# Attention turned MoE layer on one core: q of chunks 2 and 3 turned by the DMA crossbar, transposes in two halves, loads planned behind them, and token statistics summed over whole rows

## The chip, the cores and the metric

The kernel runs on one core of a Trainium2 chip. A core has a matrix engine (TensorE, PE in the profile) with its weight loads (PEld), a vector engine (VectorE, DVE), an activation engine (ScalarE, ACT), a general engine (GpSimd, POOL) and a queue engine (SyncE, SP). They run side by side, each through its own list of instructions in order, and wait for each other through semaphores. Sixteen DMA engines move data; loads here are issued on POOL (queue q0), stores and transposes on SP (queue q1). Matrix products go to PSUM, which has eight banks; everything else lies in SBUF. The metric is the time of one execution on the device in microseconds (us).

## The reference

```python
kv  = einsum('bhsd,bhse->bhde', k, v)           # b=8, h=8, s=576, d=64
o   = einsum('bhsd,bhde->bhse', q, kv)
x   = o / sqrt(mean(o*o, -1) + 1e-6) * g_norm   # per head; then [4608 tokens, 512]
h   = x @ w_in                                  # 512 -> 1024
u   = h * softmax(h)
ln  = (u - mean(u)) / sqrt(var(u) + 1e-6) * g_ln
out = ln @ w_out                                # 1024 -> 512
```

Inputs and output are float32. The layer norm needs, for each token, the mean of u, of u*u, and of exp(h), which is the softmax's divisor.

## The kernel before

The 4608 tokens are cut into nine chunks of 512. Chunk c, for c from 0 to 7, is the first 512 tokens of batch c; chunk 8 takes the last 64 tokens of all eight batches. All work on a chunk has the tokens in the columns and the features in the partitions:

1. The loads of k, v and q of a batch (`load_kv` L216, `load_q` L223), issued on POOL, cast to bfloat16 on the way. Chunks 0 and 1 load in two groups of heads, later chunks in one DMA each for k, v and q. The tiles have three buffers each. `load_q_last` (L229) fetches the last 64 tokens of a batch's q for chunk 8.
2. `kv_mm` (L278): 48 matmuls for k'v of all heads, into a bank of tag `misc`, of which there is one; four casts (L291, L293) copy the result to `kvd`, twice.
3. q has to be turned, so that head dimensions lie in the partitions. Chunks 0 to 3 do this on TensorE (`qT_mm` L301, a group of eight transposes for each half of the heads, followed by a copy out of PSUM, L310 or L308). Chunks 4 to 8 (`XBAR`, L124) are turned by the crossbar of the DMA engines (`q_turn` L315), with one instruction for all eight heads, issued on SP.
4. `o_mm` (L330) for each half of the heads, then a square, a mean over the head by TensorE (`s_mm` L351), logarithm and exponential on ACT (L355, L359) and the product x (L372, DVE).
5. `h_mm` (L449): eight groups of four 512-column matmuls; for each an exp (L457, ACT), u (L464, DVE) and u squared (L475 on POOL or L473 on ACT); for each pair of groups the sum of two exps, `es` (L481, POOL).
6. `sums` (L515): for the token statistics TensorE multiplies u, u squared and es with a column selector `stat_sel` of 32 columns, and adds them up over the features. The 128x128 array is used as four tiles of 32 columns. Each tile adds up its own 128 tokens: 20 sources of 512 columns, cut in four, make 80 matmuls of 128 columns. `sums_turn` (L523) turns the 128x128 result in 32x32 blocks within the same bank, `stats` (L531 to L536) forms the variance and `rstd` (L540, L542) its inverse root.
7. `out_mm` (L563): eight groups of four matmuls, for each of four blocks of 128 tokens two groups (halves of the features), into banks of tag `out` (two of them; `o` in part of chunk 8). `scale` (L573 DVE, L571 ACT) multiplies by rstd and `store` (L582) writes 256 KB from SP, from a tile `ob` with four buffers.

The order of the work is not written out as loops. Every piece is added to a `Plan` (L19) with its engine, an estimated length, a rank, the pieces that it needs and the buffers that it uses. `Plan.order` (L33) takes, again and again, the piece that could start earliest by those estimates (ties by rank), and the instructions are issued in that order, engine by engine. It models the load queue (`queue`, `lanes`) and the tiling in which TensorE stands; a change of tiling costs 0.1 us in it. The estimates decide the order alone; on the chip only semaphores for real data and buffers make an engine wait. In particular the list `behind` (L252) of a load names pieces of work that the load is planned after, although it shares no data with them: it decides where the load's instructions stand in POOL's list, and nothing more.

Before the change, the loads of chunk 3 are planned behind h_mm(0,2), and those of chunk b from 4 on behind h_mm(b-3,0). The lists that come out of it are quoted here as far as they are needed. On POOL: k_2 ... v_2 ... q_2 usq(0,5) k_3 v_3 es(0,1) q_3 es(0,2) es(0,3) k_4 v_4 q_4, then the twelve pieces of chunk 1 up to es(1,3), k_5 v_5 q_5 q_last(0), and further on k_6 behind es(2,3), k_7 behind es(3,3). On TensorE: kv_mm(3) stands behind h_mm(1,1), kv_mm(4) behind h_mm(2,3), kv_mm(5) behind h_mm(2,5), kv_mm(6) behind h_mm(3,4) and kv_mm(7) behind h_mm(4,4); o_mm(7,0) behind h_mm(5,6).

Of the kernel before, what the change touches and what calls it, by code (L numbers as in the profile page):

```python
# [8 lines left out]
FP32 = mybir.dt.float32  # L9
# [9 lines left out]
class Plan:  # L19
# [13 lines left out]
    def order(self):  # L33
# [3 lines left out]
        behind = {}  # L37
# [5 lines left out]
        while ready:  # L43
# [20 lines left out]
            if engine == "pe":  # L64

                tiling = n[0] if n[0] in ("kv_mm", "o_mm", "sums") else "full"
                length += 0.1 if mode.get(engine, tiling) != tiling else 0.0
                mode[engine] = tiling
            if n[0] == "qT" and engine == "sp":

                if queue > t + 1.0:
                    length, queue = 2.2 * length, queue + 2.0
            free[engine] = t + length
# [15 lines left out]
def kernel(  # L89
# [33 lines left out]
    banks = {"h": 2, "out": 2, "o": 2, "s": 1, "misc": 1}  # L123
    XBAR = tuple(range(4, NC))  # L124
    bufs = {
        "k": 3, "v": 3, "q": 3, "qT": 3, "osq": 4, "lss": 2, "rst": 2, "oc": 2, "x": 2, "e": 4, "u": 2, "usq": 2, "es": 2,
        "ob": 4,
    }
# [4 lines left out]
    def tile_of(key, shape, dtype):  # L133
        return sb.tile(shape, dtype, name=key[0] + "_sb", tag=key[0], bufs=bufs[key[0]])
# [20 lines left out]
    ident = big.tile([128, 128], BF16, name="ident")  # L155
    eye = big.tile([NF, NF], FP32, name="eye")
    zeros = big.tile([128, 512], BF16, name="zeros")
    nc.vector.memset(zeros, 0.0)  # L158
# [46 lines left out]
    def make_ident():  # L205
        make_identity(nc, ident)
        make_identity(nc, eye)

    plan.add("ident", "pool", 1.0, -1.95, make_ident)


# [38 lines left out]
    for b in range(B):  # L250
        at = b - 9.0 if b > 1 else (-2.0, -1.5)[b]
        behind = [] if b < 2 else [("h_mm", 0, 0)] if b == 2 else [("h_mm", b - 3, 2 if b == 3 else 0)]  # L252
        for g, hs in enumerate(heads(b)):
# [57 lines left out]

    def q_turn(c):

        t = T["qT", c] = tile_of(("qT", c), [128, H, 2, 128], BF16)
        nc.sync.dma_start_transpose(  # L315
            t.rearrange("q h y p -> q (h y) p"), T["q", c].rearrange("p h j d -> p (h j d)")
        )
# [61 lines left out]
    for c in range(NC):  # L379
# [14 lines left out]
        if c in XBAR:  # L394
            plan.add(("qT", c), "sp", 4.0, r - 0.1, lambda c=c: q_turn(c),
                     [("q", c, 0)] if c < B else [("q_last", b) for b in range(B)],
                     uses=[("q", c)] if c < B else [], first=[("qT", c)])
        for hf in range(2):
            g = group(c, hf)
            tag = ("out", "h")[c] if c < 2 and hf else "o"  # L400
            if c not in XBAR:
# [9 lines left out]
            plan.add(("o_mm", c, hf), "pe", 0.25 if c < B else 1.2, r + w * (0.35 + 0.5 * hf),  # L411
                     lambda c=c, hf=hf, tag=tag: o_mm(c, hf, tag), [("qT", c) if c in XBAR else ("qT", c, hf), *kvs],
                     uses=[("qT", c)], first=[(tag, c, hf, z) for z in range(2)])
# [92 lines left out]
    def sums(c, part):  # L506
        if part == 0:
            T["sum", c] = bank(("misc" if c else "h", "sum", c), [128, 2, 128], FP32)
        i, src = ((1, T["u", c]), (0, T["usq", c]), (2, T["es", c]))[part]
        n_src = NF // 2 if part == 2 else NF  # L510
        for n in range(n_src):
            for j in range(4):

                cols = src[:, n, :].rearrange("p (m j r) -> p j m r", m=4, j=4)[:, j]
                nc.tensor.matmul(  # L515
                    T["sum", c][32 * j:32 * j + 32, 0, :], stat_sel[:, i, :], cols, start=(part == 0 and n == 0),
                    stop=(part == 2 and n == n_src - 1), tile_position=(0, 32 * j), skip_group_check=True,
                )

    def sums_turn(c):  # L520

        T["st", c] = T["sum", c][:, 1, :].rearrange("p (m i) -> p m i", m=4)
        nc.vector.transpose(T["sum", c][:, 1, :], T["sum", c][:, 0, :])  # L523

    small = ctx.enter_context(tc.tile_pool(name="small", bufs=2))

    def stats(c):

        st = T["st", c]
        w = small.tile([128, 4, 3], FP32, name="w")  # L530
        nc.vector.tensor_tensor(out=w[:, :, 1:3], in0=st[:, :, 1:3], in1=factors[:, :, :], op=MUL)  # L531
        nc.vector.memset(w[:, :, 0:1], 1.0)
        terms = small.tile([128, 4, 3], FP32, name="terms")
        nc.vector.tensor_tensor(out=terms[:, :, :], in0=st[:, :, 0:3], in1=w[:, :, :], op=MUL)
        T["vare", c] = small.tile([128, 4], FP32, name="vare")
        nc.vector.tensor_reduce(out=T["vare", c][:, :], in_=terms[:, :, :], op=ADD, axis=mybir.AxisListType.X)  # L536
# [51 lines left out]
    for c in range(NC):  # L588
# [3 lines left out]
                 uses=[("u", c), ("usq", c), ("es", c)], first=[("misc" if c else "h", "sum", c)])  # L592
        plan.add(("turn", c), "dve", 0.25, rs + 0.14, lambda c=c: sums_turn(c), [("sums", c)],
                 uses=[("misc" if c else "h", "sum", c)])
        plan.add(("stats", c), "dve", 0.65, rs + 0.16, lambda c=c: stats(c), [("turn", c)], uses=[("misc" if c else "h", "sum", c)])
        plan.add(("rstd", c), "act", 0.45, rs + 0.17, lambda c=c: rstd(c), [("stats", c)])
# [45 lines left out]
```

## Time and profile before

| | |
|---|---|
| Time, median of 3 runs (lowest to highest) | 203.02 us (202.76 to 203.15) |
| The profiled execution, its own time | 203.15 us |
| Its span, first to last instruction | 201.3 us |
| PE, DVE, ACT, POOL busy | 89%, 60%, 70%, 64% |
| Granted TensorE clock | 1.0 throughout |
| HBM read, written | 32.51 MB, 9.44 MB |
| h_mm and out_mm, a group of four matmuls | 0.86 us in the chain |
| sums of a chunk (80 matmuls) | 1.23 us in the chain |
| transpose of a chunk by the crossbar, issue to landing | 3.6 to 6.6 us, median 3.9 |
| loads k, v, q of a whole chunk, issue to landing, medians | 11.8, 12.2, 13.8 us |

Times in the profile count from the first instruction. Busy time counts an engine's own instructions; issuing a DMA does not count on SP, and on POOL it does. A row of a timeline has start, length, engine, line, operation, tiles and count, and in brackets the idle time ahead of it with what ended it. A wait that hangs on several semaphores is put down to the one that came last by the profile; where the engine named had long been done, it was something else, often a DMA. The chain of waits is followed from the last instruction back: at each step to what released it, or to its predecessor on the same engine.

### The profile page before, as it was taken

What the parts mean: (1) busy time and instruction counts of PE and PEld (TensorE: products, weight loads), DVE (VectorE), ACT (ScalarE), POOL (GpSimd) and SP (SyncE); (2) the same over time, 40 slices, a digit from 0 to 9 for tenths busy, and PEclk for the clock granted to TensorE, in tenths of its full rate; (3) what the DMA queues carried; (4) which work ended last, traced back from release to release, by engine and by line L of the source; (5) the groups of instructions that cost most, each with busy time, mean ns of one, the idle gap of its engine ahead of it and who ended that gap; (6) DMA issues with size and microseconds to landing.
All of it is one profiled execution on the core that took longest, in us unless ns stands there. A gap on an engine that the chain in (4) does not pass through costs nothing.

```text
span 201.3 us, 5003 instructions
## 1 busy us (share of the span) xinstructions
PE 179.0 (89%) x2055; PEld 88.5 (44%) x2082; DVE 121.1 (60%) x232; ACT 140.9 (70%) x244; POOL 128.7 (64%) x137
## 2 busy tenths in 40 slices
PE   7987988797699889995999499999999999999990
PEld 2342444454354454453445244544545554454440
DVE  1246577468765758747484657586574748656440
ACT  2038887897698699885688558779697677655421
POOL 7962699602699984877497748397655738857200
PEclk9999999999999999999999999999999999999999
DMA  2999999999994999599849983137021111211205
GB/s 38 184 198 282 328 200 202 201 211 246 238 193 65 212 196 234 123 175 226 212 67 174 228 212 70 42 81 185 27 99 57 55 55 52 104 55 52 106 22 190
DMA packets 39990, 29.68 MB, mean 147 GB/s; under 512 B 11800, under 2 KB 34336, under 8 KB 39968
## 3 DMA queue, kind: packets, MB, share of 16 engines
q0 software_dynamic: 24208, 17.30, 56.0%
q1 hardware_dynamic: 15472, 11.54, 18.5%
q10 hardware_dynamic: 288, 0.52, 0.8%
q8 instruction: 16, 0.26, 0.5%
q14 instruction: 6, 0.05, 0.1%
HBM read 32.51 MB, written 9.44 MB: 208 GB/s over the span
## 4 chain that ended last, share of the span: by engine, by line
PE 55%; DMA 23%; ACT 7%; POOL 6%; issue 4%; DVE 3%; POOLq 0%; ACTq 0%
PE out_ps L563 22%; PE h_ps L449 20%; DMA v_sb<-in_v_dram 15%; DMA w_out_f<-in_moe_w_out_dram 9%; PE misc_ps L515 4%; PE o_ps L330 2%; PE s_ps L351 2%; PE misc_ps L278 2%; PE o_ps L563 2%; ACT e_sb L457 2%; POOL k_sb L216 2%; ACT rst_sb L359 1%; ACT lss_sb L355 1%; DVE u_sb L464 1%; ACT osq_sb L345 1%
## 5 line engine op out<-in xcount | busy, mean ns | idle before, releaser
L449 PE MATMUL h_ps<-x_sb,w_in_sb 128*128 128x512 bf16 x264 | 69.0, 379 | 2.2 <-DVE x_sb L372 1.2
L563 PE MATMUL out_ps<-w_out_sb,u_sb 128*128 128x512 bf16 x259 | 66.9, 379 | 1.4 <-issue 0.8
L481 POOL TENSOR_TENSOR es_sb<-e_sb 128x512 bf16<-128x512 f32 x36 | 45.7, 1270 | 34.5 <-ACT e_sb L457 34.3
L464 DVE TENSOR_TENSOR u_sb<-h_ps,e_sb 128x512 bf16<-128x512 f32 x69 | 47.3, 687 | 29.4 <-ACT e_sb L457 28.9
L475 POOL TENSOR_TENSOR usq_sb<-u_sb 128x512 bf16<-128x512 bf16 x51 | 52.6, 1042 | 18.5 <-DVE u_sb L464 18.2
L457 ACT ACTIVATE e_sb<-h_ps,zero_t 128x512 f32<-128x512 f32 x69 | 47.1, 685 | 15.3 <-PE h_ps L449 15.0
L449 PEld LDWEIGHTS <-w_in_sb 128*128 128x128 bf16 x288 | 27.3, 98 | 34.7 <-issue 3.6
L563 PEld LDWEIGHTS <-u_sb 128*128 128x128 bf16 x288 | 27.1, 98 | 32.4 <-issue 1.4
L372 DVE SCALAR_TENSOR_TENSOR x_sb<-o_ps,g_rep,rst_sb 128x512 bf16<-128x512 f32 x32 | 24.0, 750 | 9.3 <-ACT rst_sb L359 8.9
L573 DVE TENSOR_SCALAR ob_sb<-out_ps,rstd 128x512 f32<-128x512 f32 x33 | 24.4, 745 | 8.4 <-ACT rstd L542 4.7
L345 ACT ACTIVATE osq_sb<-o_ps,zero_t 128x512 bf16<-128x512 f32 x31 | 19.8, 682 | 7.6 <-PE o_ps L330 7.6
L359 ACT ACTIVATE rst_sb<-lss_sb,zero_t 128x512 f32<-128x512 f32 x32 | 23.3, 728 | 0.6
L355 ACT ACTIVATE lss_sb<-s_ps,eps_t 128x512 f32<-128x512 f32 x32 | 22.0, 688 | 0.8 <-PE s_ps L351 0.7
L473 ACT ACTIVATE usq_sb<-u_sb,zero_t 128x512 bf16<-128x512 bf16 x21 | 15.2, 722 | 5.4 <-DVE u_sb L464 5.2
L293 ACT CAST kvd<-misc_ps 64x128 bf16<-64x128 f32 (+1 forms) x24 | 7.5, 313 | 15.1 <-DVE kvd L291 10.8
L351 PE MATMUL s_ps<-osq_sb,head_mean 128*128 128x512 bf16 x34 | 12.9, 380 | 0.9 <-ACT lss_sb L355 0.6
L278 PE MATMUL misc_ps<-v_sb,k_sb 96*64 96x64 bf16 x384 | 8.0, 197 | 6.0 <-DMA v_sb<-in_v_dram 3.7
L515 PEld LDWEIGHTS <-stat_sel 128*32 128x32 bf16 x720 | 10.2, 97 | 4.3 <-issue 4.3
L278 PEld LDWEIGHTS <-k_sb 96*64 96x64 bf16 x384 | 7.1, 112 | 10.7 <-issue 10.7
L197 PE MATMUL s_ps<-zeros 128*128 128x512 bf16 x27 | 10.1, 502 | 1.6 <-DVE zeros L158 1.2
L223 POOL DMA_DIRECT2D q_sb<-in_q_dram x10 | 8.5, 853 | 3.5 <-DMA w_in_sb<-in_moe_w_in_dram 1.5
L291 DVE CAST kvd<-misc_ps 64x256 bf16<-64x256 f32 (+1 forms) x16 | 6.1, 382 | 6.8 <-ACT kvd L293 4.8
(80 smaller groups left out, 127.4 us busy)
## 6 DMA issues: line engine op xcount, KB each, us to landing
out_dram<-ob_sb SPq DMA_DIRECT2D x34, 256.0 KB, 2.5
k_sb<-in_k_dram POOLq DMA_DIRECT2D x6, 576.0 KB, 11.8
v_sb<-in_v_dram POOLq DMA_DIRECT2D x6, 576.0 KB, 12.2
q_sb<-in_q_dram POOLq DMA_DIRECT2D x6, 512.0 KB, 13.8
w_out_f<-in_moe_w_out_dram POOLq DMA_DIRECT2D x1, 2048.0 KB, 17.6
k_sb<-in_k_dram POOLq DMA_DIRECT2D x4, 288.0 KB, 12.4
v_sb<-in_v_dram POOLq DMA_DIRECT2D x4, 288.0 KB, 12.7
q_sb<-in_q_dram POOLq DMA_DIRECT2D x4, 256.0 KB, 12.7
```

What stands on the lines that cost most here:

```text
L278: nc.tensor.matmul(t[hh * 64:hh * 64 + 64, n, :], T["k", b][:, h, i, :], T["v", b][:, h, i, :], start=(n == 0 and i == 0), stop=(i == 5), ...
L345: nc.scalar.activation(out=t[:, :], in_=T[("o", *i)].rearrange("p a b c -> p (a b c)"), func=AF.Square, bias=zero_t[:, :])
L355: nc.scalar.activation(out=t[:, :], in_=T["s", i][:, :], func=AF.Ln, bias=eps_t[:, :])
L359: nc.scalar.activation(out=t.rearrange("p a b c -> p (a b c)"), in_=T["lss", i][:, :], func=AF.Exp, scale=-0.5, bias=zero_t[:, :])
L372: nc.vector.scalar_tensor_tensor(out=T["x", c][:, 2 * hf:2 * hf + 2, z], in0=T["o", c, hf, z][:, :, :, :], scalar=g_rep[:, :], in1=T["rst" ...
L449: nc.tensor.matmul(t[:, :], w_in_sb[:, dt, f * 128:(f + 1) * 128], T["x", c][:, dt].rearrange("p a b c -> p (a b c)"), start=(dt == 0), st ...
L457: nc.scalar.activation(out=T["e", c, f // 2][:, f % 2, :], in_=T["h", c, f][:, :], func=AF.Exp, bias=zero_t[:, :])
L464: nc.vector.tensor_tensor(out=T["u", c][:, f, :], in0=T["h", c, f][:, :], in1=T["e", c, f // 2][:, f % 2, :], op=MUL)
L475: nc.gpsimd.tensor_tensor(out=dst, in0=src, in1=src, op=MUL)
L481: nc.gpsimd.tensor_tensor(out=T["es", c][:, n, :], in0=e[:, 0, :], in1=e[:, 1, :], op=ADD)
L563: nc.tensor.matmul(T["acc", c, m][:, :], T["u", c][:, f, m * 128:(m + 1) * 128], w_out_sb[:, f, :], start=(f == 0), stop=(f == NF - 1),)
L573: nc.vector.tensor_scalar_mul(out=t[:, :], in0=T["acc", c, m][:, :], scalar1=T["rstd", c][:, m:m + 1])
```

## The change

It has three parts.

*Turning q.* `XBAR` begins at chunk 2 instead of 4, so the TensorE transposes and copies of chunks 2 and 3 fall away. Each crossbar transpose is cut in two, one for heads 0 to 3 and one for heads 4 to 7 (128x8x128 elements instead of 128x16x128), and `o_mm` of a half needs its own half alone. The planner's length of a transpose goes from 4.0 to 2.0 for a half, and one that meets a busy load queue now pushes that queue by its own length.

*The loads.* From chunk 3 on, the loads of chunk b are planned behind the first half of the transpose of chunk b-1, and, from chunk 4 on, h_mm(b-3,0).

*The statistics.* `sums` gives each of the four 32-column tiles whole sources of 512 columns in turn, 20 matmuls instead of 80. The four tiles then hold partial sums of the same tokens. `sums_turn` turns 128x512 in 32x32 blocks from PSUM to a new SBUF tile `sumT`, and a new piece `stats_mm` (`st_mm` in the plan) adds up the four parts: four float32 matmuls with 32 output rows and 12 columns each, with a constant `fold` of four stacked 32x32 identities. `stats` reads their bank, and so waits for TensorE once more.

```diff
             if n[0] == "qT" and engine == "sp":
                 if queue > t + 1.0:
-                    length, queue = 2.2 * length, queue + 2.0
+                    length, queue = 2.2 * length, queue + length
...
-    XBAR = tuple(range(4, NC))
+    XBAR = tuple(range(2, NC))
...
+    def make_fold():
+        for j in range(4):
+            nc.vector.tensor_copy(fold[32 * j:32 * j + 32, :], ident[32 * j:32 * j + 32, 32 * j:32 * j + 32])
...
-        behind = [] if b < 2 else [("h_mm", 0, 0)] if b == 2 else [("h_mm", b - 3, 2 if b == 3 else 0)]
+        behind = [] if b < 2 else [("h_mm", 0, 0)] if b == 2 else [("qT", b - 1, 0)] + ([("h_mm", b - 3, 0)] if b > 3 else [])
...
-    def q_turn(c):
-        t = T["qT", c] = tile_of(("qT", c), [128, H, 2, 128], BF16)
+    def q_turn(c, hf):
+        if hf == 0:
+            T["qT", c] = tile_of(("qT", c), [128, H, 2, 128], BF16)
+        hs = slice(4 * hf, 4 * hf + 4)
         nc.sync.dma_start_transpose(
-            t.rearrange("q h y p -> q (h y) p"), T["q", c].rearrange("p h j d -> p (h j d)")
+            T["qT", c][:, hs].rearrange("q h y p -> q (h y) p"), T["q", c][:, hs].rearrange("p h j d -> p (h j d)")
         )
...
         for n in range(n_src):
-            for j in range(4):
-                cols = src[:, n, :].rearrange("p (m j r) -> p j m r", m=4, j=4)[:, j]
-                nc.tensor.matmul(
-                    T["sum", c][32 * j:32 * j + 32, 0, :], stat_sel[:, i, :], cols, start=(part == 0 and n == 0),
-                    stop=(part == 2 and n == n_src - 1), tile_position=(0, 32 * j), skip_group_check=True,
-                )
+            j = n % 4
+            nc.tensor.matmul(
+                T["sum", c][32 * j:32 * j + 32, :], stat_sel[:, i, :], src[:, n, :],
+                start=(part == 0 and n < 4), stop=(part == 2), tile_position=(0, 32 * j), skip_group_check=True,
+            )
     def sums_turn(c):
-        T["st", c] = T["sum", c][:, 1, :].rearrange("p (m i) -> p m i", m=4)
-        nc.vector.transpose(T["sum", c][:, 1, :], T["sum", c][:, 0, :])
+        t = T["sumT", c] = tile_of(("sumT", c), [128, 4, 4, 32], FP32)
+        nc.vector.transpose(t.rearrange("p a b c -> p (a b c)"), T["sum", c][:, :])
+
+    def stats_mm(c):
+        t = T["st", c] = bank(("misc", "st", c), [128, 4, 3], FP32)
+        for g in range(4):
+            nc.tensor.matmul(
+                t[32 * g:32 * g + 32, :, :], fold[:, :], T["sumT", c][:, :, g, 0:3],
+                start=True, stop=True, tile_position=(0, 32 * g),
+            )
...
-            plan.add(("qT", c), "sp", 4.0, r - 0.1, lambda c=c: q_turn(c),
+            for hf in range(2):
+                plan.add(("qT", c, hf), "sp", 2.0, r - 0.1 + 0.01 * hf, lambda c=c, hf=hf: q_turn(c, hf),
...
+        plan.add(("st_mm", c), "pe", 0.15, rs + 0.15, lambda c=c: stats_mm(c), ["fold", ("turn", c)],
+                 uses=[("sumT", c)], first=[("misc", "st", c)])
```

The lists that come out of it: on POOL, usq(0,5) es(0,1) es(0,2) es(0,3) k_3 v_3 q_3, then the twelve pieces of chunk 1, q_last(0), k_4 v_4 q_4; k_5 behind es(2,3) and q_last(2), k_6 behind es(3,3), k_7 behind usq(4,5). On SP: store(0,0) store(0,1) qT(2,0) qT(2,1) store(0,2) store(0,3) qT(3,0) qT(3,1), and so on. On TensorE: o_mm(2,0) behind h_mm(1,1), kv_mm(3) behind h_mm(1,6), kv_mm(4) behind h_mm(2,5), kv_mm(5) behind h_mm(3,5), kv_mm(6) behind h_mm(4,4), kv_mm(7) behind h_mm(5,3); o_mm(7,0) behind h_mm(5,6). A piece st_mm(c) stands one group of h_mm or out_mm behind sums(c), in some chunks with an o_mm besides.

## The prediction

> **What bounds the kernel now.** I read the page's summary first, then its chain of waits.
>
> ```profile
> PE 179.0 (89%) x2055; PEld 88.5 (44%) x2082; DVE 121.1 (60%) x232; ACT 140.9 (70%) x244; POOL 128.7 (64%) x137
> PE   7987988797699889995999499999999999999990
> DMA  2999999999994999599849983137021111211205
> PE 55%; DMA 23%; ACT 7%; POOL 6%; issue 4%; DVE 3%; POOLq 0%; ACTq 0%
> ```
>
> TensorE leads, but a slice is 5 us, and only from slice 23 on (114 us) is PE solid. Before that DMA is full or nearly so, and 23% of the chain is DMA. So two stages: up to 114 us loads decide, after it TensorE. The chain in order of time shows how a load decides:
>
> ```profile
> 101.12 0.69 POOL es_sb L481
> 101.81 0.53 issue
> 102.33 0.82 POOL k_sb L216
> 103.16 10.55 DMA v_sb<-in_v_dram
> 113.85 0.95 PE misc_ps L278 x48
> ```
>
> Chunk 7's loads stand on POOL behind the last `es` of chunk 3. k is issued at 102.33, v lands 11.4 us later, and TensorE, which runs in order, waits at `kv_mm`. TensorE's timeline prices that:
>
> ```profile
> 46.10 0.41 PE L330 MATMUL o_ps<-qT_sb,kvd 64*64 64x256 bf16 x8
> 93.41 0.95 PE L278 MATMUL misc_ps<-v_sb,k_sb 96*64 96x64 bf16 x48 [2.08 <-DVE u_sb L464]
> 113.85 0.95 PE L278 MATMUL misc_ps<-v_sb,k_sb 96*64 96x64 bf16 x48 [2.47 <-DMA v_sb<-in_v_dram]
> ```
>
> The 2.08 us named after u_sb is chunk 6's v: issued at 83.10, landing 10.2 later (93.3). From k's issue to v's landing it took 11.0 (chunk 6) and 11.4 (chunk 7); chunk 5, 10.4. The row at 46.10 is chunk 2's first `o_mm`, which matters below. Last, what the SP queue meets: its stores between 41 and 56 us, its transposes, and who moved packets from 45 to 47 us.
>
> ```profile
> L582 SPq DMA_DIRECT2D out_dram<-ob_sb x4: 332/332/384, 41.3 to 47.5; - x4
> DMA to landing us min/median/max: 6.6/6.8/6.9
> ...
> DMA to landing us min/median/max: 3.6/3.9/6.6
> ...
> q1 hardware_dynamic: 213, 0.40, 64.1%
> q0 software_dynamic: 217, 0.17, 54.0%
> ```
>
> A store under the load stream lands after 6.6 to 6.9 us (2.5 is the page's median). The second landing row is the whole-chunk transposes; all five were issued after chunk 4's q had landed (63.0), so the load stream never stood in front of one. In the last two rows the two queues share packet by packet.
>
> **What the skill says.** The Trainium skill, "DMA: Bandwidth & Descriptors", section on queues, rings and completion order: an engine takes its queues in turn, packet by packet, and consumes one ring in order. The trace agrees (213 to 217). "VectorE: DVE Perf Modes", the three transpose paths: crossbar 1309 ns for one 128x128 block, TensorE 390. Sixteen blocks here land in 3.6 us, about 1.85 us of it packets (118.2 to 120.1); the trace decides. "TensorEngine Tiling (Array Packing)", key properties: a change of tiling drains TensorE. Here 0.16 us of issue stands after each `sums` or `o_mm`, and about 0.1 ahead. "FP8 and Floating Point Precision", TensorE precision notes: a true FP32 product takes four passes; nothing here shows one at this shape.
>
> **The change, part by part.**
>
> *q of chunks 2 and 3 by the crossbar.* Gone: 32 TensorE transposes (four groups, 0.45 to 0.6 us) and four DVE copies of 0.69. In place of a wait of TensorE, `o_mm(2,0)` now waits for a DMA. q of chunk 2 was issued at 27.79 and landed 14.6 later, at 42.4. The first half stands on SP behind stores 0_0 and 0_1 (41.32, 41.98), in the same ring. Chunk 3's loads are planned behind that half, but on POOL only their place moves, no semaphore ties them: they come after es_0_1 to es_0_3, so at 29.8 + 3 x 1.25 = 33.6 instead of 29.74. They are in the queue when the half goes out. The two stores landed at 48.2 and 48.8, their packets ending near 48. Then 1024 packets of the half, 64 per DMA engine, alternate with load packets: half of 1.85 us is 14.5 ns each, a load packet takes 60 ns (k, v: 48 per engine in 2.9 us) or 40 (q): about 31 x 74.5 + 33 x 54.5 ns = 4.1 us, so 52.2 landed. Bounds: 49.3 if the half goes through at its own speed (0.93 us plus the receipt); 53.5 if all pairs are with k or v packets. I take 52.2. PE arrives at `o_mm(2,0)` behind h_mm(1,1) at about 47.7: it stalls 4.5 us, with h_mm(1,2) and everything after it queued behind.
>
> *Chunk 4's loads.* Before, they were issued from 35.93 (in hand long before use). Now they stand where chunk 5's did, behind es_1_3, usq_1_7 and a q_last. From `o_mm(2,0)`: 0.4 for it, 17 ACT operations of 0.6 and two casts of 0.37 (11.0), 0.8 of gaps, es 1.25, usq 1.0, q_last 0.55: 15.0. So k at 67.2, and with 11.2 (chunks 6, 7) v and `kv_mm(4)` at 78.4. The DMA queues idle meanwhile from some 56.
>
> *Chunks 5, 6, 7.* Each load moves one chunk later on POOL, each `kv_mm` too, so the wait I saw twice now comes four times. Period 4 to 5: kv 0.95, casts one after another 1.6, five ACT operations 3.0, es and q_last 1.8, load 11.2: 18.5. 5 to 6: kv, one s_mm and five groups 5.5, exp 0.7, es 1.25, load 11.2: 18.7. 6 to 7: kv 0.95, casts 1.6, three ACT operations 1.8, es and usq 2.25, load 11.2: 17.8. TensorE's own work in each is 17.3 (15 groups of 0.865, four s_mm, two o_mm, sums, st_mm, kv), so loads bind and hide the new statistics work here. `kv_mm(7)`: 78.4 + 55.0 = 133.4; with it and one s_mm done, 134.6. The same work was complete before at 132.4. **+2.2.**
>
> *o_mm(7,0).* q lands 3.3 after v, a half takes some 2.7 from issue; PE arrives after 5.5 of work: **+0.5.** Before, it had a chunk of slack (landed 120.7, used 135.1).
>
> *sums, turn, st_mm.* 80 matmuls of 128 columns took 1.23 us, 15.4 ns each against 54 alone, so four column tiles overlap; 20 of 512 columns are five deep at 0.216: 1.08 (4.3 if they didn't overlap, which 15.4 speaks against). The turn: 0.328 at 128 columns and 1.02 ns a column (casts: 284 ns at 128, 415 at 256), 0.72 at 512; PE runs a group of 0.87 meanwhile. st_mm: between 0.25 (16 passes at 15.4 ns) and 1.1 (four of the page's f32 matmul at 0.271); I take 0.3, plus 0.26 for two switches. Net +0.4 a chunk. Chunks 5 to 8 lie in the solid stage: **+1.6.** At the end, rstd comes about 1 us later, under five groups of out_mm (4.3): nothing.
>
> Sum +4.3 on the profiled execution: span 201.3 to 205.6, its run 203.15 to 207.4. The median of the runs is 0.13 lower, 203.02, so **207.3**.
>
> **Rivals.** *Through at its own speed*: the half lands at 49.3, all after it 2.9 earlier, net +1.4: 204.4. For it: a ring might pass small packets in bunches. Against: the alternation at 45 to 47. *The statistics cost TensorE more*: st_mm near its upper bound, or waiting on the turn behind u in the two chunks with just 0.97 us between: up to +0.8 more in four chunks, so 210.5. Against: DVE stood waiting for sums (5 waits, 7.0 us), so it is prompt. *Faster, the loads land earlier*: at each of four loads v takes 9.5 instead of 11.2 after k's issue. `kv_mm(4)` gains 1.7, the three periods fall to TensorE's 17.3 (3.1 in all): -0.5, 202.5. It decides below about 9.7. For it: a k and v in the running stream take 5.8 of transfer, and chunk 5 had 10.4. Against: chunks 6 and 7 from an idle queue had 11.0 and 11.4, as all four would be. *The change doesn't do what it says*: the loads aren't held back behind the half; that is part of my forecast, not apart from it.
>
> **How the numbers follow.** Forecast 0.54 (its own range 205.3 to 209); through at its own speed 0.18; dearer statistics 0.10; loads earlier 0.14; about equal, where a shorter stall and cheap statistics meet, 0.04. 0.2% (0.4 us) is about what a measurement of this kernel can tell from no change. So faster 0.14, same 0.04, slower 0.82. From 202.6 the range holds the equal and the slower cases, up to 210.0, which takes in most of the dearer statistics; it leaves out the faster case and a little more, under 0.2.
>
> **What would show it.** In the profile after: chunk 2's first half landing 7 us or more after issue, and PE idle some 4 us ahead of chunk 2's o_mm; chunk 4's k issued near 67; waits for v ahead of four kv_mm; sums at 1.1 us with st_mm about one group behind; TensorE solid after chunk 7's kv_mm. The prediction is wrong if the half lands by 49, if chunk 4's k goes out before 64, or if the kv_mm of chunks 5 to 7 don't wait: then PE, not the loads, sets the middle.

## The result, and the profile after

The changed kernel takes 210.73 us (median of 4 runs, 209.86 to 211.59); the kernel before took 203.09 us beside it on the same chip (202.76 to 204.17). The ratio is 1.037, 95% interval 1.031 to 1.042: slower by about 7.6 us, where 4.3 was forecast. The ratios in this document leave out executions that took over 1.5% more than the fastest of the same kernel, so they can differ by some tenths of a per cent from the ratio of two medians. The profiled execution took 210.62 us, its span is 208.8 us against 201.3, and its mean granted TensorE clock 0.964 against 1.0.

First the page of the changed kernel: the busy sums, three of its rows of 40 slices (here 5.2 us each), and the shares of the chain that ended last.

```profile
PE 184.0 (88%) x1557; PEld 81.9 (39%) x1582; DVE 123.0 (59%) x232; ACT 142.3 (68%) x244; POOL 129.0 (62%) x137
PE   7987979790599599999999799999999999999990
PEclk9999999998579789999999999999999999999998
DMA  4999999999920099989969999989212111202206
PE 63%; DMA 20%; DVE 4%; ACT 4%; POOL 4%; issue 2%; POOLq 0%; SPq 0%; ACTq 0%
```

Three things are new. PE has a hole at its tenth and eleventh digit, 47 to 57 us. The clock row, which was 9 throughout before, falls to 5 in that hole, and once more to 7 behind the smaller hole at 68 to 73 us. And the DMA row, full up to there, shows "200": the DMA engines stand idle from 59 to 72 us. After that, PE is nearly as solid as it was from slice 23 on before.

The chain in order of time (start, length, engine, what) shows what the hole hangs on:

```profile
42.48 11.96 DMA qT_sb<-q_sb
54.48 0.64 PE o_ps L339 x8
55.12 1.82 PE h_ps L459 x4
```

The first half of chunk 2's q is issued to the crossbar at 42.48 and lands 12.0 us later. Before, no transpose took over 6.6 us. TensorE's timeline, with the idle time in brackets:

```profile
54.48 0.64 PE L339 MATMUL o_ps<-qT_sb,kvd 64*64 64x256 bf16 x8 [7.08 <-DMA qT_sb<-q_sb]
55.05 1.89 PE L459 MATMUL h_ps<-x_sb,w_in_sb 128*128 128x512 bf16 x4
63.48 0.41 PE L339 MATMUL o_ps<-qT_sb,kvd 64*64 64x256 bf16 x8
63.82 1.04 PE L459 MATMUL h_ps<-x_sb,w_in_sb 128*128 128x512 bf16 x4
118.33 0.95 PE L285 MATMUL misc_ps<-v_sb,k_sb 96*64 96x64 bf16 x48 [1.35 <-DMA v_sb<-in_v_dram]
135.59 0.95 PE L285 MATMUL misc_ps<-v_sb,k_sb 96*64 96x64 bf16 x48
141.58 0.41 PE L339 MATMUL o_ps<-qT_sb,kvd 64*64 64x256 bf16 x8 [0.41 <-DMA qT_sb<-q_sb]
```

`o_mm(2,0)`, at 46.10 before, comes at 54.48, after a wait of 7.08 us. The same group of four h matmuls takes 1.89 us right behind the wait and 1.04 us nine microseconds later. The stretches of the trace give the clock (the column of 1.00, 0.66, 0.50 behind POOL; then the DMA share and GB/s):

```profile
48.00:50.00 2.00, 0.00 (x0) 0.00 (x0) 0.74 (x2) 0.12 (x1) 1.86 (x2) 1.00 1.52 131
50.00:51.00 1.00, 0.00 (x0) 0.00 (x0) 0.00 (x0) 0.00 (x0) 1.00 (x2) 0.66 1.34 182
51.00:52.00 1.00, 0.00 (x0) 0.00 (x0) 0.00 (x0) 0.00 (x0) 0.39 (x1) 0.50 1.35 184
59.00:60.00 1.00, 1.00 (x4) 0.33 (x3) 0.17 (x1) 0.89 (x2) 0.69 (x2) 0.50 0.00 0
60.00:61.00 1.00, 1.00 (x4) 0.35 (x3) 1.00 (x2) 0.99 (x2) 1.00 (x1) 0.72 0.00 0
```

TensorE fell idle at 47.4 (54.48 less 7.08). The clock dropped to one half 2.9 us later (0.66 over the microsecond from 50 is 0.32 us at full and the rest at half clock, so the step is at 50.32) and came back at 60.56, 6 us after work had resumed. This is the state that the Trainium skill, "TensorE: Matmul & The Clock Gate", Part 1, describes: after an idle window of about 3.4 us, half rate. The trace agrees on the fall, after 2.9 us here. It took longer than the page's 3.4 us of work to rise again.

The steps themselves show why. The smaller hole has two more, read in the same way: down at 70.80, up at 74.22. From step to step it is 10.24, 10.24 and 3.42 us, which is three, three and one times 3.41. Cut into stretches of 3.41 us at these steps, the trace reads (the second number is TensorE's busy time):

```profile
46.91:50.33 3.42, 0.49 (x3) 0.10 (x1) 1.39 (x2) 1.09 (x2) 2.19 (x2) 1.00 1.41 171
50.33:53.74 3.41, 0.00 (x0) 0.00 (x0) 0.00 (x0) 0.00 (x0) 1.05 (x2) 0.50 1.35 165
53.74:57.15 3.41, 2.67 (x13) 0.93 (x13) 0.00 (x0) 1.38 (x3) 0.00 (x0) 0.50 1.18 234
57.15:60.56 3.41, 3.41 (x9) 1.22 (x8) 1.42 (x3) 2.60 (x5) 1.72 (x2) 0.50 0.52 103
```

The stretch with 0.49 us of work was followed by half clock. The one in which work resumed, with 2.67 us of it, did not bring full clock back; the next, busy throughout, did. The other traces read the same way (see the last section).

One reading makes all kernels here comparable. From `o_mm(7,0)` on, TensorE never waits for a load again, and what is left takes 61.31 us with the old statistics (135.09 to 196.40 in the kernel before) and 62.24 us with the new ones (141.58 to 203.82). It is so within 0.01 us in every kernel below whose order there is the same. So a kernel's time is told by when `o_mm(7,0)` starts. Here: 6.49 us later than before, and then 0.93 us for the statistics of four chunks.

### The profile page after: what moved, and what is told of

The parts are those of the page before. It is cut to its first block, busy times and chain, and to the rows that moved or that the text cites. A ratio compares the mean times of both kernels' runs of the same rounds, so it can differ in the third digit from the quotient of the medians.

```text
span 208.8 us, 4013 instructions
## 1 busy us (share of the span) xinstructions
PE 184.0 (88%) x1557; PEld 81.9 (39%) x1582; DVE 123.0 (59%) x232; ACT 142.3 (68%) x244; POOL 129.0 (62%) x137
## 4 chain that ended last, share of the span: by engine, by line
PE 63%; DMA 20%; DVE 4%; ACT 4%; POOL 4%; issue 2%; POOLq 0%; SPq 0%; ACTq 0%
PE h_ps L459 24%; PE out_ps L580 23%; DMA w_out_f<-in_moe_w_out_dram 8%; DMA qT_sb<-q_sb 7%; DMA v_sb<-in_v_dram 5%; PE misc_ps L523 4%; PE s_ps L360 3%; PE o_ps L339 3%; DVE w_out_sb L571 3%; PE misc_ps L285 2%; PE o_ps L580 2%; POOL k_sb L223 1%; PE out_ps L565 1%; ACT e_sb L467 1%; ACT osq_sb L354 1%
## 5 line engine op out<-in xcount | busy, mean ns | idle before, releaser
L459 PE MATMUL h_ps<-x_sb,w_in_sb 128*128 128x512 bf16 x265 | 72.7, 396 | 2.1 <-DVE x_sb L381 1.4
L459 PEld LDWEIGHTS <-w_in_sb 128*128 128x128 bf16 x288 | 28.0, 101 | 37.9 <-issue 9.7
L339 PE MATMUL o_ps<-qT_sb,kvd 64*64 64x32 bf16 (+1 forms) x240 | 8.5, 265 | 7.7 <-DMA qT_sb<-q_sb 7.5
L360 PE MATMUL s_ps<-osq_sb,head_mean 128*128 128x512 bf16 x34 | 13.5, 397 | 0.3 <-ACT osq_sb L354 0.2
L339 PEld LDWEIGHTS <-kvd 64*64 64x64 bf16 x256 | 4.6, 116 | 14.9 <-issue 14.0
L223 POOL DMA_DIRECT2D k_sb<-in_k_dram x10 | 7.8, 778 | 3.7 <-DMA w_in_sb<-in_moe_w_in_dram 2.2
## 6 DMA issues: line engine op xcount, KB each, us to landing
w_out_f<-in_moe_w_out_dram POOLq DMA_DIRECT2D x1, 2048.0 KB, 17.3
```

What stands on the lines that cost most here:

```text
L360: nc.tensor.matmul(t[:, :], head_mean[:, :], T["osq", i][:, :], start=True, stop=True)
L459: nc.tensor.matmul(t[:, :], w_in_sb[:, dt, f * 128:(f + 1) * 128], T["x", c][:, dt].rearrange("p a b c -> p (a b c)"), start=(dt == 0), st ...
```

## Experiments

The runs stand on three chips, on which the kernel before has medians of 205.10, 205.17 and 204.65 us. So each ratio is to the kernel before on the same chip, and mechanisms are read inside one trace. In the table, "wait" is that of TensorE ahead of `o_mm(2,0)`; the last column is from the profiled execution.

| kernel | median, us | ratio to before (95%) | wait, us | o_mm(7,0) starts |
|---|---|---|---|---|
| before | 203.09 | 1 | 0 | 135.09 |
| changed kernel | 210.73 | 1.037 (1.031 to 1.042) | 7.08 | 141.58 |
| crossbar from chunk 4 | 201.49 | 0.989 (0.980 to 0.999) | 0 | 132.12 |
| crossbar from chunk 3 | 204.13 | 0.997 (0.993 to 1.001) | 0 | 134.90 |
| loads really wait for the half | 204.67 | 0.995 (0.992 to 0.998) | 0 | 137.07 |
| loads as planned before | 205.34 | 1.006 (1.003 to 1.010) | 2.09 | 137.51 |
| matmuls on zeros in the wait | 209.04 | 1.020 (1.017 to 1.023) | 0.89 | 139.15 |
| whole transposes | 216.86 | 1.055 (1.042 to 1.068) | 0 | other order |
| changed, old statistics | 212.57 | 1.038 (1.028 to 1.049) | 6.52 | 147.02 |
| before, new statistics | 201.44 | 0.987 (0.980 to 0.994) | 0 | 132.23 |
| before, kv_mm planned later | 201.04 | 0.977 (0.971 to 0.983) | 0 | 133.08 |
| before, earlier loads | 201.40 | 0.988 (0.980 to 0.997) | 0 | 133.52 |
| earlier loads, new statistics | 200.12 | 0.980 (0.973 to 0.987) | 0 | 130.70 |

Those of the old statistics in the changed kernel, of the loads as planned before and of the loads that wait were profiled in executions 1.2 to 2.4 us above their medians; their last column may be late by as much.

After the result my theory had three parts: the transposes of chunk 2 share the DMA engines with chunk 3's loads, so TensorE stands; its clock falls; and the new statistics cost the rest. Rivals: the statistics are the larger part; or the loads that start late are the cause by themselves. (The expectations speak of a "mark after kv_mm(7)" at 132.4 in the kernel before. That is two groups too late, as told further on.)

**The crossbar from chunk 4 again**, all else as changed.

```diff
-    XBAR = tuple(range(2, NC))
+    XBAR = tuple(range(4, NC))
```

> Chunks 2 and 3 turn q on TensorE again; halves, the planned order of the loads and the new statistics stay. Stall theory (the transposes of chunk 2 share the DMA engines with chunk 3's loads, TensorE stands 7 us at o_mm of chunk 2, and its clock falls after that): no wait above 1 us at o_mm(2,0), the granted clock near 1 between 54 and 61 us, the mark after kv_mm(7) back from 136.7 to about 132.5, and 206.5 us in all (205.5 to 207.5), since only the statistics remain. Statistics theory (they are the larger part): 209.5 or more. Load-order theory (the loads that start one step later are the cause by themselves): the stall is gone, but kv_mm of 4 to 7 still come late, mark near 136, 210 us.

The wait is gone, and not only that: 0.989, below the kernel before. So turning chunks 2 and 3 by the crossbar costs 1.037 - 0.989, 4.8% or some 9.7 us, more than the whole loss (what it does to the planner's order is in that figure). What is left of the change gains about 1%, so the statistics can't be the larger part, and the 206.5 that I had for this kernel (they "remain" as a cost) is wrong. Nor are late loads the cause by themselves: here chunk 4's k is issued at 60.47, against 35.93 in the kernel before, TensorE waits for v just once, 1.13 us, and the kernel is not slower.

**The old statistics in the changed kernel, and the new ones in the kernel before.** In the first, `sums`, `sums_turn` and the planned lengths are those of before and the folding matmul is out; in the second only they are new:

```diff
-            for j in range(4):
-                cols = src[:, n, :].rearrange("p (m j r) -> p j m r", m=4, j=4)[:, j]
...
+            j = n % 4
+            nc.tensor.matmul(
+                T["sum", c][32 * j:32 * j + 32, :], stat_sel[:, i, :], src[:, n, :],
...
+        plan.add(("st_mm", c), "pe", 0.15, rs + 0.15, lambda c=c: stats_mm(c), ["fold", ("turn", c)],
```

> The changed kernel with the sums, the turn and the statistics of the kernel before (no folding matmul). Stall theory: the wait of about 7 us at o_mm(2,0), the low clock behind it and the mark near 136.5 all stay; only the stretch after the mark shrinks, from 72 to 69 us, so 207.5 us (206.5 to 208.5). Statistics theory: 204 us or less.

> The kernel before with the new sums, turn and folding matmul alone. Stall theory: mark as before, within 0.7 us of 132.4 (what chunks 0 to 3 lose lies in waits for v), the stretch after it 72 instead of 69 us: 206.0 us (205 to 207). Statistics theory: 209 us or more, nearly all of the loss of the changed kernel. My blind sum, 0.4 us per chunk for four chunks: 204.7.

Both expectations fell. Without the new statistics the changed kernel is no faster (1.038 against 1.037), and with them alone the kernel before gets faster by 1.3%. Yet on TensorE they do cost: 62.24 instead of 61.31 us from `o_mm(7,0)` on. The gain lies ahead of it. The kernel before waited 2.08 and 2.47 us at the kv_mm of chunks 6 and 7. With the new statistics the planner, whose estimates had changed, put these two behind 64 and 80 groups of h_mm and out_mm instead of 49 and 65. The timeline of that kernel has kv_mm(6) without a wait, 14.3 us later than at 93.41 before, and the folding matmul that it now passes:

```profile
106.36 0.25 PE L534 MATMUL misc_ps<-sumT_sb,fold 128*32 128x12 f32 x8
106.55 1.04 PE L577 MATMUL out_ps<-w_out_sb,u_sb 128*128 128x512 bf16 x3
107.42 0.38 PE L358 MATMUL s_ps<-osq_sb,head_mean 128*128 128x512 bf16 x1
107.73 0.95 PE L285 MATMUL misc_ps<-v_sb,k_sb 96*64 96x64 bf16 x48
```

**The kernel before with only the plan touched**, to test that reading: kv_mm of chunks 6 and 7 need two more pieces, which moves them behind 64 and 80 groups. No instruction is added or taken away.

```diff
-                         [("k", c, g), ("v", c, g)], uses=[("k", c), ("v", c)], first=[("misc", "kv", c, g)])
+                         [("k", c, g), ("v", c, g)] + {6: [("sums", 3)], 7: [("o_mm", 6, 1)]}.get(c, []), uses=[("k", c), ("v", c)], first=[("misc", "kv", c, g)])
```

> The kernel before, with nothing but the plan touched: kv_mm of chunks 6 and 7 need sums of chunk 3 and o_mm(6,1), and so stand some 20 places later in TensorE's order, about where they stand in the kernel that has the new statistics alone. Order theory (the new statistics gained 1.9 us only because their planned costs moved kv_mm behind the landing of v): the two waits of 2.1 and 2.5 us go, nothing else changes, 199 us (198.3 to 200.5). Rival (the new sums are themselves cheaper on TensorE): no gain here, or the waits return in another place; 202.5 us or more.

0.977: the gain is all there, by the ratios rather more than with the new statistics (0.987; the intervals touch). Its kv_mm of chunks 6 and 7:

```profile
109.78 0.95 PE L278 MATMUL misc_ps<-v_sb,k_sb 96*64 96x64 bf16 x48
127.57 0.95 PE L278 MATMUL misc_ps<-v_sb,k_sb 96*64 96x64 bf16 x48
```

Neither waits. The execution of it whose mean clock was 1.0 spans 197.3 us, the one of the new statistics at clock 1.0 spans 199.5, with almost the same order: 2.2 us, 0.24 for each of nine chunks. That is one execution of each, on two chips, but it agrees with 0.93 us for four. The two waits may not be all that the kernel before loses: in its profile the clock was 1.0 throughout, but in 21 of 23 executions of one series its mean was 0.977 to 0.994. Which waits cost it clock there is not on record.

**The loads as planned before**, in the changed kernel.

```diff
-        behind = [] if b < 2 else [("h_mm", 0, 0)] if b == 2 else [("qT", b - 1, 0)] + ([("h_mm", b - 3, 0)] if b > 3 else [])
+        behind = [] if b < 2 else [("h_mm", 0, 0)] if b == 2 else [("h_mm", b - 3, 2 if b == 3 else 0)]
```

> The changed kernel, but the next chunks' loads are issued where the kernel before issues them and not behind the first half. Stall theory: chunk 3's loads are in the queues during the transposes in both, so the wait at o_mm(2,0) stays at 6 to 9 us and the time at 209 to 212 us. Load-order theory: the loads no longer come a step late, kv_mm of 4 to 7 come 4 us earlier, 206 to 207 us.

1.006, nearer to the load-order theory, but not for its reason alone: the wait at `o_mm(2,0)` is 2.09 us, not the 6 to 9 that I expected. The half is as slow (issued 41.85, landed 52.45, 10.6 us), but the plan now puts kv_mm(3) ahead of `o_mm(2,0)`, and TensorE gets there later:

```profile
49.46 0.95 PE L285 MATMUL misc_ps<-v_sb,k_sb 96*64 96x64 bf16 x48 [0.40 <-DMA v_sb<-in_v_dram]
52.50 0.64 PE L339 MATMUL o_ps<-qT_sb,kvd 64*64 64x256 bf16 x8 [2.09 <-DMA qT_sb<-q_sb]
```

It changes two things at once, so it does not tell the late loads from the wait.

**Loads that really wait.** In the changed kernel chunk 3's loads are planned behind the half, but no semaphore ties them to it; they were issued at 33.5, nine microseconds ahead of it. Here a copy of one column on GpSimd reads the turned half, and the loads stand behind that copy in POOL's list.

```diff
-        behind = [] if b < 2 else [("h_mm", 0, 0)] if b == 2 else [("qT", b - 1, 0)] + ([("h_mm", b - 3, 0)] if b > 3 else [])
+        behind = [] if b < 2 else [("h_mm", 0, 0)] if b == 2 else ["hold" if b == 3 else ("qT", b - 1, 0)] + ([("h_mm", b - 3, 0)] if b > 3 else [])
...
+    def hold():
+        t = big.tile([128, 1], BF16, name="held")
+        nc.gpsimd.tensor_copy(t[:, :], T["qT", 2][:, 0, 0, 0:1])
+
+    plan.add("hold", "pool", 0.1, -8.0, hold, [("qT", 2, 0)], uses=[("qT", 2)])
```

> The changed kernel with one tiny GpSimd copy that reads the first half of chunk 2's turned q; chunk 3's loads are issued behind that copy, so they really wait for the half instead of only standing behind it in the plan. Sharing theory (packets of chunk 3's loads in the queues make the halves late): the half lands by 50 us, about 3 us after the stores ahead of it, the wait at o_mm(2,0) falls from 7.1 to 2.5 us or less, and the run comes to 206 us (204 to 208). Rival (the place in the ring behind the stores and the small packets cost the time by themselves): it still lands after 53 us, wait 6 to 7 us, 210 us or more.

The half lands 4.8 us after its issue (42.33 to 47.14), the wait is gone, and the time is 204.67. Sharing is the cause, and the place behind the stores by itself is not. But the place counts under sharing: the second store landed 7.2 us after the half's issue in the changed kernel and 3.8 us after it here, so of the 7.15 us that the half gains, 3.34 lie in the stores ahead and 3.81 in its own packets. Who moved packets from 49 to 52 us in the changed kernel, and then from 43 to 47 us in this one (packets, MB, share of 16 engines):

```profile
q0 software_dynamic: 696, 0.36, 86.2%
q1 hardware_dynamic: 701, 0.18, 46.4%
```

```profile
q1 hardware_dynamic: 1610, 0.60, 71.7%
```

One packet of the loads for one of the transposes in the first, none in the second. The price of holding the loads back appears too: TensorE's waits of this kernel (total, times, longest) name v at three kv_mm, and two of these waits, of 1.64 and 1.62 us, were each followed by 3.4 us at half clock (60.08 to 63.50 and 94.22 to 97.62).

```profile
PE misc_ps L285 <- DMA v_sb<-in_v_dram: 4.4, 3, 1.6
```

**Transposes in one piece**, without halves.

```diff
-            for hf in range(2):
-                plan.add(("qT", c, hf), "sp", 2.0, r - 0.1 + 0.01 * hf, lambda c=c, hf=hf: q_turn(c, hf),
+            for hf in range(1):
+                plan.add(("qT", c, hf), "sp", 4.0, r - 0.1, lambda c=c, hf=hf: q_turn(c, hf),
...
-        hs = slice(4 * hf, 4 * hf + 4)
+        hs = slice(0, 8)
...
```

> The changed kernel with q turned in one piece per chunk and not in two halves. If the halves hardly matter for the stall (both were issued within 2.4 us and ended within 1 us of each other): the piece lands near 55.5, TensorE waits 7 to 8 us at o_mm(2,0), as before. By the plan's costs the later loads and kv_mm all come some ten groups later, so 211 us or more. If the halves are what makes the turn slow: it lands by 51, wait 4 us or less, 207 us or less.

Neither theory had both: no wait at `o_mm(2,0)`, and yet 216.86 us. The plan set chunk 3's loads further back in POOL's list, where they were issued at 48.78, so the transpose met none, and all eight heads landed in 5.8 us (42.16 to 47.95), half the time that four heads took beside the loads. It is the test above once more, by accident. Then v is late at every chunk from 3 on:

```profile
PE misc_ps L285 <- DMA v_sb<-in_v_dram: 13.1, 5, 4.6
```

So the plan has two ways to lose here: loads in the queue slow the transpose, and loads held back for it leave TensorE without v. Since the order moved as well, this run does not price the halves by themselves.

**TensorE kept busy in the wait.** 26 matmuls on zeros, 5.8 us, ahead of `o_mm(2,0)`; their product is not used.

```diff
+    plan.add(("warm", "x"), "pe", 0.1, -5.0, lambda: warm(26, "misc"), [("h_mm", 1, 0)], first=[("misc", "warm", "x")])
```

> The changed kernel with 26 matmuls on zeros (their product is thrown away) put into TensorE's wait ahead of o_mm(2,0), 5.6 us of work. Clock theory (TensorE stood idle, so its clock was lowered): PEclk stays at 9 throughout 54 to 62 us, the nine us from o_mm(2,0) to o_mm(2,1) become 6, and 207.7 us (206.5 to 208.5). Rival (the clock falls for another reason, or the 3 us are hidden by later waits for loads): the groups after o_mm(2,0) take 1.7 us as now, or the gain is gone by kv_mm(4); 210 us or more.

The timeline of this kernel:

```profile
47.34 5.78 PE L198 MATMUL misc_ps<-zeros 128*128 128x512 bf16 x26
54.01 0.41 PE L339 MATMUL o_ps<-qT_sb,kvd 64*64 64x256 bf16 x8 [0.89 <-DMA qT_sb<-q_sb]
54.35 1.04 PE L460 MATMUL h_ps<-x_sb,w_in_sb 128*128 128x512 bf16 x4
60.92 0.41 PE L339 MATMUL o_ps<-qT_sb,kvd 64*64 64x256 bf16 x8
```

The half lands as late (53.97), but the clock stays at 1.00 over 54 to 63 us, a group takes 1.04 as ever, and `o_mm(2,1)` comes 6.9 us after `o_mm(2,0)` instead of 9.0. Idleness is what took the clock. The gain is 1.7% by the ratios, and 2.4 us at `o_mm(7,0)`. The median, 209.04, lies half a microsecond above the range I gave, but on a chip where the kernel before takes 205.17 us; 1.020 times 203.09 would be 207.1. A later wait of 2.39 us, and 3.4 us at half clock behind it, are in both kernels (68.66 to 72.08 here, 70.80 to 74.22 in the changed kernel).

**The crossbar from chunk 3**, so that chunk 2 alone is on TensorE.

```diff
-    XBAR = tuple(range(2, NC))
+    XBAR = tuple(range(3, NC))
```

> The changed kernel with chunk 2 turned on TensorE and the crossbar from chunk 3 on. If chunk 2 alone is what costs (its turn meets chunk 3's loads, which are in the queues already, while chunk 3's turn comes when they are empty): no wait above 1 us at o_mm of chunks 2 and 3, and 200.5 to 202 us, no slower than the version from chunk 4. If any turn before chunk 4 costs: a wait of 3 us or more at o_mm(3,0), 205 us or more.

No wait at `o_mm` of chunks 2 or 3: chunk 3's halves are issued at 53.45 and 54.85, when its q has just landed and no other load is queued, and land 3.4 and 3.2 us later. But 204.13 us, between what the two expected: the loads of chunks 4 to 7, planned behind the transposes, come late, and TensorE waits for v:

```profile
PE misc_ps L285 <- DMA v_sb<-in_v_dram: 3.5, 2, 1.8
```

So of the 4.8% that the crossbar costs in chunks 2 and 3, 4.0 belong to chunk 2 (1.037 - 0.997). Whether chunk 3 costs the other 0.8 is not settled; the intervals of 0.989 and 0.997 overlap.

**A better kernel than both.** The two waits for v could also be met from the other side: in the kernel before the loads are issued half a chunk earlier, first without and then with the new statistics.

```diff
-        behind = [] if b < 2 else [("h_mm", 0, 0)] if b == 2 else [("h_mm", b - 3, 2 if b == 3 else 0)]
+        behind = [] if b < 2 else [("h_mm", 0, 0)] if b == 2 else [("h_mm", 0, 2) if b == 3 else ("h_mm", 1, 0) if b == 4 else ("h_mm", b - 4, 4)]
```

> The kernel before with the loads of chunks 4 to 7 issued half a chunk earlier (behind h_mm(1,0) and the fifth h_mm of chunk b-4 instead of the first of chunk b-3), all else as it was; the plan then also sets kv_mm of 6 and 7 later. Load theory (what is left to gain in the kernel before is waits for v): no wait for v at chunks 6 and 7, as with kv_mm planned later: 0.977 of the kernel before, 199 to 201.5 us on a chip where that takes 203 to 205. Rival (earlier loads collide with stores and with the turns of chunks 4 and 5): new waits at o_mm(4,0) or o_mm(5,0), 0.99 or more.

> The same earlier loads, with the new statistics. With the waits for v gone in both, what is left between this and the run without them is what the new statistics cost on TensorE: 0.23 us for each of nine chunks by the traces so far (four chunks after o_mm(7,0) took 62.24 instead of 61.31 us), so 1 to 2 us more than without. If they gain by themselves: the same or less.

0.988 and 0.980. No wait for v is left at chunks 6 and 7 in either. In the first, a pause of 2.25 us inside kv_mm(5), which the profile puts down to issue and nothing else, is followed by 3.4 us at half clock (77.34 to 80.76); I don't know its cause. It also spoils the comparison of the two: the new statistics came out 1.3 us ahead instead of 1 to 2 behind. The second, at 199.72 to 200.40 us, and the kernel with only kv_mm planned later both beat the two kernels of this case; their intervals (0.980 and 0.977) overlap.

## Why the prediction was off

The direction, and the mechanism that starts it, were right: a packet-by-packet share with chunk 3's loads, TensorE standing at `o_mm(2,0)`, then chunk 4's loads late. The sizes were not, and one term had the wrong sign. In the forecast's own terms, the half and so `o_mm(2,0)` came 2.3 us later than forecast, `o_mm(2,0)` to the k took 2.8 us more, and a misread mark hid 1.7; the other way went the loads (0.4 up to `kv_mm(4)`, 2.5 in the three periods) and the statistics (0.7). That makes 3.1 of the 3.4 us by which it fell short (210.73 less 207.3). The largest failed step is the second: TensorE's work behind the wait was reckoned at full clock.

| step | predicted | measured |
|---|---|---|
| first half lands | 52.2 | 54.44 |
| wait at o_mm(2,0) | 4.5 | 7.08 |
| o_mm(2,0) to chunk 4's k | 15.0 | 17.8 |
| k to v, chunks 4 to 7 | 11.2 each | 9.6, 9.2, 10.9, 10.6 |
| kv_mm(4) to kv_mm(7) | 55.0 | 52.5 |
| kv_mm(7) | 133.4 | 135.59 |
| wait at o_mm(7,0) | 0.5 | 0.41 |
| statistics, four chunks | 1.6 | 0.93 |

*"The first half lands at 52.2."* Late by 2.2. The two stores ahead landed at 49.16 and 49.65, a microsecond later than before. From 49 to 52 us the 701 packets make 44 an engine, 68 ns a pair, close to the 54 to 74 that I had used. The rest is probably the other half, issued 2.3 us behind the first on the same ring: when the loads' packets thinned out near 52, the two together drained at 890 packets in 2 us. With 701 packets by 52 and 497 in the next microsecond, the first half's 1024 would have been through at 52.7 if they had gone ahead of the other's; it landed at 54.44. No run tests this. My upper bound of 53.5 took neither into account. I had also passed over a sign in the kernel before, where I wrote that the load stream never stood in front of a transpose: chunk 4's, issued at 63.08 with chunk 5's loads 0.4 us behind it, took 6.63 us, those of chunks 6 and 7, with no k, v or q in the queues, 3.87 and 3.64.

*"15.0 from o_mm(2,0) to the k."* This is the step that failed most plainly. I counted operations at full clock. TensorE's work from `o_mm(2,0)` to `o_mm(2,1)` took 9.0 us, and 6.9 where the clock had been kept. In that kernel the k came 15.7 after `o_mm(2,0)` (54.01 to 69.69) instead of 17.8 us, so 2.1 of the 2.8 us are clock. The Trainium skill, "TensorE: Matmul & The Clock Gate", Part 1, states that an idle window of about 3.4 us brings half rate; I had forecast 4.5 us of idleness and put its effect on the clock at nothing.

*"The loads bind."* Only chunk 6's kv_mm waited, 1.35 us; at chunk 4 v had landed at 81.80 and TensorE came at 83.05. This is the sign that the prediction itself had named: TensorE, not the loads, set the middle. Its three periods took 52.5 us, 17.5 each, against the 17.3 that I had for its own work. The rival of earlier loads had its mechanism right (9.2 to 10.9 us instead of 11.2), but what it gained in the periods, 2.5 us, was less than the wait and the clock cost. That a load with no store inside its time is the quick one (9.2 us for chunk 5, none issued between k's issue and v's landing) is argued from the trace alone.

*"The same work was complete before at 132.4."* A plain misreading. In the kernel before, h_mm(5,4), which follows that work, starts at 130.68; 132.40 is h_mm(5,5), two groups further. By my own numbers the middle should have been +3.9, not +2.2, and the sum +6.0. With it the forecast would have been 209.0: 1.7 of the 3.4 us. That the remainder is so small is in part luck, since the wait and the clock (5.1 us too little) and the loads (2.9 too much) go against each other.

*The statistics.* By the terms: a chunk costs 0.23 us on TensorE, not 0.4. The sums from their first matmul to the `o_mm` behind take 2.16 instead of 2.20 us, and the folding matmul 0.2 to 0.3 with its switches. (The 0.16 us of issue that I read after each `sums` or `o_mm` in the kernel before stands there eight times in all.) DVE's turn took 0.71 as forecast, and rstd at the end was indeed free. But as a part of the change they gain in the kernel before, because their estimates move kv_mm of chunks 6 and 7. I had seen those two waits and read them as the price of late loads. They were just as much the price of kv_mm planned too early.

The other rivals: "through at its own speed" fell (12.0 us, not 7), and so did "dearer statistics". That the loads aren't held back by a plan's order alone was right: issued at 33.49.

What stays open: why the changed kernel does not profit when the new statistics are taken out of it, although TensorE has 0.93 us less to do; four waits for v, 7.5 us in total, stand in its profile, where v of chunks 4 and 5 took 11.7 and 12.5 us from k's issue instead of 9.6 and 9.2, but that execution took 2.4 us more than the median. The stall, the clock and the late loads are not independent, so their shares do not add up: removing the sharing is worth 4.2%, removing the crossbar of chunks 2 and 3 is worth 4.8%.

## What to carry over

Before a step is moved from an engine to DMA, look at what else is in the DMA queues from its issue to its landing. A plan's order delays a load only by the work that stands ahead of it on its engine; to keep it out of the queue takes a semaphore, and has its own price. A wait of TensorE is to be priced twice, once as the wait and once as half clock behind it, in stretches of 3.41 us: here a wait of 7.1 us cost three of them, and some waits of 1.6 to 2.5 us cost one or more. Where a planner sets the order, an edit to one piece's estimated length can be worth more than the edit itself (here 2.3%, some 4.7 us, from moving two pieces, against the 2 us that the edit added on TensorE), so compare orders first, and test an order by itself.

## What the runs showed of the hardware

- Half a chunk's crossbar transpose (four heads) took 3.2 to 4.1 us from issue to landing in the changed kernel with no k, v or q in the queues, 4.8 behind two stores in the kernel whose loads wait, and 9.9 to 14.4 us for chunk 2's halves beside chunk 3's loads (four kernels). A whole one took 5.8 us behind two stores.
- TensorE's clock fell to 0.50 for 10.24 us after 2.9 us without work, three stretches of 3.41 us. Shorter waits did it at times: 2.45 us, ending at 55.55, in the kernel with kv_mm planned later (one stretch, 55.18 to 58.60), 2.09 us with the loads as planned before (three, 51.72 to 61.96), but not the 2.08 and 2.47 us of the kernel before or the 2.48 us of that with the new statistics.
- What goes with it is the work in a stretch. In each of the thirteen traces all steps of the clock are whole multiples of 3.41 us apart. Between 10 and 190 us the traces have 658 such stretches at full clock. The 10 with at most 1.48 us of TensorE work were all followed by half clock; of the 637 with more than 1.91 us, none was; of the 11 between, 4 were. At half clock, the 6 with at most 2.67 us of work stayed there, and the 14 with 3.04 us or more went back to full. So a wait that lies across a step of this grid is shared by two stretches: the 2.08 us of the kernel before left 2.29 and 2.40 us of work in its two, while the 2.45 us named above lay in one nearly whole, with 1.33 us of work. This is read from the traces; no edit was made to test it.
- Twenty matmuls of 512 columns into four column tiles of 32 take about 1.2 us, as long as eighty of 128 columns. One behind the other, at the 0.216 us that such a matmul takes in a group of four (0.865 us), they would take 4.3: the four tiles work side by side.
